# Top-32 attention feeding a mixture of experts: PSUM tiles of single banks and single heads, and natural token order for the first q and k

## The chip, the core and the metric

The kernel runs on one core of a Trainium2 chip. The time is the device time of one execution in microseconds (us). The core has five engines that each work through their own instructions in order: TensorE (PE, matmuls and transposes; PEld is its weight loads), VectorE (DVE), ScalarE (ACT), GpSimd (POOL) and SyncE (SP, which issues most DMAs). They wait for one another through semaphores. Matmuls write to PSUM, eight banks of 512 fp32 numbers in each of 128 partitions; DVE and ACT read it, POOL and DMAs don't.

## What is computed

Inputs: q, k, v of 2 batches, 8 heads, 576 tokens and 64 channels, a gate of 512 x 8, and the two weight matrices of 8 experts (512 x 1024 and 1024 x 512).

```python
scores = scale * np.matmul(q, k.transpose(0, 1, 3, 2))
kth = np.partition(scores, -top_k, axis=-1)[..., -top_k:-top_k + 1]     # top_k = 32
scores = np.where(scores >= kth, scores, -1e9)
attn = np.exp(scores - np.max(scores, axis=-1, keepdims=True))
x = (attn / attn.sum(-1)) @ v        # as 1152 tokens of 512 channels
e = np.argmax(x @ w_gate, axis=1)    # one expert for each token, at most 288 tokens each
out[i] = softmax(x @ w_gate)[i, e] * (np.maximum(x[i] @ w1[e], 0) @ w2[e])
```

## The kernel before

**Units.** The 1152 tokens make 9 blocks of 128. A unit `u` is one block and one pair of heads, 36 in all. For each unit PE makes two heads' scores of 128 x 576 (`scores`, L267); DVE takes the 8 largest of nine segments of 64 in each head (`heads`, L284) and finds from them a bound near the 32nd largest (`merge`, `bound`, L298 and L322); ACT writes the shifted scores to SBUF (`shift`, L332), which frees the scores' PSUM; ACT counts with a sign (`sign`), POOL multiplies (`turn`), DVE picks the exact threshold (`select`, L368); ACT makes a penalty for scores below it (`penalty`, L384); PE transposes scores and penalty together and ACT takes the exponential (`probs`, L393, three pieces: four 128 x 128 blocks of each head, and the last 64 columns of both heads as one block, in the tile pTt); PE multiplies with v into the tile pV (`values`, L417) and DVE divides (`normalise`).

**The order** in each engine is the order of the Python calls: the kernel schedules by hand. In the loop of `attention` (L989) iteration `i` runs `heads` and `merge` of unit `i`, `probs` of `i-3`, `values` of `i-4` and `scores` of `i+1`, so the units overlap. `routes` adds the routing steps of finished blocks (`route`, L470: transposes, gate logits, the token's expert and slot, and a scatter of the token to DRAM).

**PSUM.** The eight banks are: pD (small DVE work), pT (two buffers of one bank: transposes), pTt (one bank), pV (one bank) and pS, one tile of three banks (L270) that holds both heads' scores one behind the other, 1152 of 1536 columns. When a tile is written while another engine still has reads of it open, the writer waits; for pS the three banks count as one tile, and the next unit's scores are written when the shift of both heads has ended. At the start and in the experts the same tile serves as three banks: `tail_p` (L458) gives them out for the first transposes and the last routing, and `take_banks` (L807) puts them with pT, pD and pV into a list of seven, of which `bank` gives the next in turn.

**The start** (L121 to L176 and L1155 to L1176). SP loads q and k by pairs of heads. For the first two pairs a partition takes six successive tokens, 1,536 bytes in one piece; for the others it takes tokens 96 apart, six pieces of 256 bytes (L93). The numbers are split into a high and a low fp16 half (`split_qk`), transposed on PE (`trans_pe`) and copied to SBUF (`take`, L231) by ACT or DVE; for the first two pairs the copy also puts the tokens back in order (L234), with an output step of six elements.

**The experts** (L825). After the attention, the leftover tokens of the two fullest experts ("r", 64 each), then the other six experts in order of size: 192, 176, 144, 128, 128 and 128 tokens (L864). For each: the first layer by groups in one bank each (`h_of`), ACT's relu into `hh` (L712, L771), DVE's low half `hl` (L721, L772), the second layer (`small_y`, `ffn`), and a scatter of the result. Between the groups ACT and DVE split the next expert's weights into halves (`split_w`, L582: ACT L588, DVE and POOL L594), and SP loads further ones as buffers come free.

Of the kernel before, what the change touches and what calls it, by code (L numbers as in the profile page):

```python
# [19 lines left out]
FT = mybir.dt.float32  # L20
# [14 lines left out]
def kernel(  # L35
# [11 lines left out]
    nc = tc.nc  # L47
# [16 lines left out]
    def open_pool(key):  # L64
        P[key] = ExitStack()
        P[key, 0] = P[key].enter_context(tc.tile_pool(name=key, bufs=2, reuse_waits="tile"))
# [19 lines left out]
    def load_qk(b, p, tag="nat", names="qk"):  # L86
        for name in names:
            src = q if name == "q" else k
            XN[name, b, p] = x = (work.tile if tag == "nat" else att)([PR, 2, R, D], FT, name=name + "nat", tag=tag, bufs=4 if tag == "nat" else 2)
            for j in range(2):  # L90
                nc.sync.dma_start(x[:, j], bass.AP(
                    tensor=src.tensor, offset=src.offset + (b * H + 2 * p + j) * S * D,
                    ap=[[D, PR], [PR * D, R], [1, D]] if b or p > 1 else [[R * D, PR], [D, R], [1, D]]))  # L93
# [137 lines left out]
    def take(p, slot, j, pt, eng):  # L231
        o, pt = qk_of(0)[slot][:, 2 * p + j], pt[:, :S]
        if p < 2:
            o, pt = o.rearrange("p (t r) -> p r t", r=R), pt.rearrange("p (r t) -> p r t", r=R)  # L234
        if eng is nc.scalar:
            eng.activation(o, pt, AF.Copy)  # L236
        else:
            eng.tensor_copy(o, pt)
# [28 lines left out]
    def scores(u):  # L267
        t, p = divmod(u, HP)

        PS[u] = psum.tile([128, 3, 512], FT, name="pS", bufs=1).rearrange("p g c -> p (g c)")  # L270
        for j in range(2):
            h = 2 * p + j
            for c0, c1 in ((0, 512), (512, S)) if j == 0 else ((0, 1024 - S), (1024 - S, S)):
                for row, n, b, s in parts(t):
                    for i in range(2):
                        nc.tensor.matmul(PS[u][row:row + n, j * S + c0:j * S + c1], QK[b][2 * i][:, h, s:s + n],  # L276
                                         QK[b][1][:, h, c0:c1], start=(i == 0), stop=(i == 1))

    def scores_of(u, j):
        return PS[u][:, j * S:(j + 1) * S]  # L280
# [134 lines left out]
    PLG, PPO = pv[:, 320:328], pv[:, 384:392]  # L415
# [54 lines left out]
    def route(t, stage, eng):  # L470
        x = XR[t]
        if stage == 0:
            if TAIL_P:
                px = TAIL_P[0].rearrange("p (c t) -> p c t", c=4)
# [418 lines left out]
    def tally(i):  # L893
        PK[i] = (psum.tile([128, 128], FT, name="pTt", bufs=1), CG[:, i])
# [41 lines left out]
    def check(step):  # L936
        if step == 1:
            pf = psum.tile([128, 128], FT, name="pTt", bufs=1)
# [14 lines left out]
    def count():  # L953
        pc = psum.tile([128, 128], FT, name="pTt", bufs=1)
# [22 lines left out]
    def warm(n, few=False):  # L977
        o = psum.tile([128, 128], FT, name="pTt", bufs=1) if few else TAIL_P[2]
# [4 lines left out]
    def attention(side, early, late, mid, act, pool, end):  # L983
# [5 lines left out]
        for i in range(NU - 1):  # L989
# [82 lines left out]
        merge(L, fill)  # L1072
        tail_p()
# [80 lines left out]
    ACT, DVE, POOL = nc.scalar, nc.vector, nc.gpsimd  # L1154
    tail_p()  # L1155
# [6 lines left out]
    pt = [psum.tile([128, 1024], HF, name=f, bufs=n) for f, n in (("pT", 2), ("pT", 2), ("pTt", 1))]  # L1162
    pt += [a.bitcast(HF) for a in TAIL_P[:2]] + [pv.bitcast(HF)]
# [5 lines left out]
    TAIL_P.clear()  # L1169
    trans_qk(0, 1, 0, ACT)  # L1170
# [53 lines left out]
    close_pool("exp")  # L1224


    with tc.If(BAD[0] > 0):
        wrong = nc.values_load(flags, min_val=0, max_val=1 << 20)
        with tc.If(wrong > 0):
            open_pool("att")  # L1230
            init_xbuf(0, E * cap // 128)
# [26 lines left out]
            open_pool("exp")  # L1258
            experts_plain(0, LEAST)
            close_pool("exp")  # L1260
        more = nc.values_load(many, min_val=0, max_val=1)
        with tc.If(more > 0):
            WS.clear()
            WHICH.clear()
            open_pool("exp")
            experts_plain(LEAST, cap - LEAST)
            close_pool("exp")

# [32 lines left out]
```

## Time and profile before

| | |
|---|---|
| median of 3 runs | 434.12 us (432.04 to 436.24) |
| the profiled execution | 433.01 us, span 431.2 us |
| busy | PE 333.1, PEld 281.3, DVE 338.4, ACT 298.1, POOL 262.4 us |
| chain that ended last | DVE 55%, PE 23%, ACT 8%, issue 6%, POOL 4% |
| start, to the first maxima on DVE | 0 to 17.6 us |
| attention units | 17.6 to about 264 us |
| last routing, first expert matmuls | 264 to 302 us |
| experts | 302 to 431 us |

Busy time is the union of an engine's instructions. A row of the order of time gives start, duration, engine, line, operation, output and input tiles, and in brackets the idle time before it and the instruction that ended the wait. A busy engine is a bound only in the stretch in which it is full; elsewhere the waits tell.

### The profile page before, as it was taken

The numbers are of one execution on the slowest core, as the hardware profiler recorded it, in microseconds if no ns is written. First come the engines' busy times: TensorE is split into PE (matmuls) and PEld (weight loads), VectorE is DVE, ScalarE is ACT, GpSimd is POOL, SyncE is SP. The second block draws the span as 40 slices with busy tenths as digits, with TensorE's granted clock in tenths as the row PEclk, the third lists the DMA queues.
The fourth block names the chain that finished last, engine by engine and source line by source line (L and its number), as shares of the span: only waits on it lengthen the run. The fifth ranks groups of instructions, "written<-read, shape, count | busy, mean of one in ns | idle before, by whom it ended". The sixth has DMA issues, their size and how long they took to land.

```text
span 431.2 us, 10457 instructions
## 1 busy us (share of the span) xinstructions
PE 333.1 (77%) x3516; PEld 281.3 (65%) x3519; DVE 338.4 (78%) x1840; ACT 298.1 (69%) x553; POOL 262.4 (61%) x288
## 2 busy tenths in 40 slices
PE   4556777787877978878687898977689878895692
PEld 2334566675776757667576788973669767883571
DVE  5648999999999999999999999954427573779430
ACT  6889898898988989888896969632328543576210
POOL 5266776778885797988879799742425230548100
PEclk9559799999999999999999999999699969899698
DMA  7034989857292900000305326389589993590000
GB/s 193 1 84 110 196 227 217 189 111 113 39 286 68 346 8 27 2 2 24 100 24 183 137 39 211 120 269 338 76 301 262 281 380 84 185 291 24 0 21 22
DMA packets 66086, 60.30 MB, mean 140 GB/s; under 512 B 47461, under 2 KB 48229, under 8 KB 66023
## 3 DMA queue, kind: packets, MB, share of 16 engines
q1 hardware_dynamic: 63879, 54.79, 45.9%
q0 software_dynamic: 1616, 4.73, 3.0%
q8 instruction: 29, 0.48, 0.4%
q14 instruction: 34, 0.28, 0.2%
q10 hardware_dynamic: 528, 0.02, 0.1%
HBM read 40.66 MB, written 12.09 MB: 122 GB/s over the span
## 4 chain that ended last, share of the span: by engine, by line
DVE 55%; PE 23%; ACT 8%; issue 6%; POOL 4%; DMA 1%; SPq 0%; POOLq 0%; DVEq 0%; ACTq 0%
DVE un L291 18%; DVE z L377 10%; PE pS L633 4%; DVE ws L594 3%; ACT ws L588 3%; ACT qk L236 3%; DVE wk L314 3%; DVE pD L308 2%; DVE wk L311 2%; PE pT L728 2%; DVE pD L318 2%; PE pT L633 2%; PE pV L433 2%; PE pS L728 2%; DVE vb L316 1%
## 5 line engine op out<-in xcount | busy, mean ns | idle before, releaser
L291 DVE MAX8 un<-pS 128x8 f32<-128x64 f32 x648 | 107.4, 217 | 4.4 <-PE pS L276 4.4
L353 POOL TENSOR_TENSOR z<-sm,sg 128x576 f32<-128x576 f32 x71 | 89.4, 1279 | 29.7 <-ACT sg L346 29.4
L633 PEld LDWEIGHTS <-ws 128*128 128x128 f16 (+1 forms) x960 | 63.2, 108 | 21.8 <-issue 18.0
L594 DVE TENSOR_TENSOR ws<-wr,ws 128x1024 bf16<-128x1024 f32 x40 | 61.4, 1561 | 17.9 <-ACT ws L588 17.9
L433 PE MATMUL pV<-vm,pT 128*128 128x65 f32 (+1 forms) x640 | 73.7, 263 | 0.0
L391 ACT ACTIVATE pen<-sm,nk 128x576 bf16<-128x576 f32 x70 | 50.6, 768 | 28.9 <-DVE nk L381 28.9
L433 PEld LDWEIGHTS pV<-vm,pT 128*128 128x128 f32 (+1 forms) x640 | 69.8, 181 | 0.8
L594 POOL TENSOR_TENSOR ws<-wr,ws 128x1024 bf16<-128x1024 f32 x24 | 57.5, 2399 | 16.3 <-ACT ws L588 14.3
L276 PE MATMUL pS<-qk 128*128 128x512 f16 (+7 forms) x320 | 43.3, 293 | 29.5 <-ACT sm L336 25.5
L409 PE MATMUL pT<-identb,pen 128*128 128x128 bf16 x288 | 54.0, 225 | 13.0 <-ACT pen L391 13.0
L408 PE MATMUL pT<-ident,sm 128*128 128x128 f32 x288 | 60.2, 288 | 3.8 <-ACT xT L499 2.4
L643 POOL DMA_INDIRECT out_dram<-y,xp x12 | 14.2, 1184 | 74.6 <-DVE y L796 31.7
L276 PEld LDWEIGHTS <-qk 128*128 128x128 f16 (+1 forms) x320 | 25.4, 105 | 48.6 <-issue 32.6
L346 ACT ACTIVATE sg<-sm,mx 128x576 bf16<-128x576 f32 x72 | 54.7, 762 | 0.0
L588 ACT ACTIVATE ws<-wr 128x2048 f16<-128x2048 f32 (+1 forms) x26 | 47.6, 1844 | 6.7 <-POOL ws L594 3.3
L377 DVE MAX8 z<-z 128x8 f32<-128x576 f32 x72 | 50.8, 747 | 0.0
L336 ACT ACTIVATE sm<-pS,mx 128x576 f32<-128x576 f32 x72 | 49.1, 733 | 0.3
L408 PEld LDWEIGHTS pT<-ident,sm 128*128 128x128 f32 x288 | 42.7, 148 | 9.0 <-ACT xT L499 3.8
L633 PE MATMUL pS<-xe,ws 128*128 128x64 f16 (+7 forms) x432 | 29.8, 242 | 19.6 <-DVE hl L721 10.7
L409 PEld LDWEIGHTS <-pen 128*128 128x128 bf16 x288 | 29.8, 106 | 18.8 <-ACT pen L391 18.7
L410 ACT ACTIVATE pT<-pT 128x512 f32<-128x512 f32 x72 | 39.2, 597 | 2.6 <-PE pT L409 2.4
L781 PEld LDWEIGHTS <-ws 128*128 128x128 f16 (+1 forms) x288 | 22.6, 101 | 2.9 <-issue 2.9
(246 smaller groups left out, 661.0 us busy)
## 6 DMA issues: line engine op xcount, KB each, us to landing
wr<-in_moe_w_dram SPq DMA_DIRECT2D x32, 1024.0 KB, 6.4
xbuf<-zero SPq DMA_DIRECT2D x6, 771.0 KB, 5.5
qnat<-in_q_dram SPq DMA_DIRECT2D x16, 144.0 KB, 3.4
knat<-in_k_dram SPq DMA_DIRECT2D x16, 144.0 KB, 3.6
out_dram<-zero SPq DMA_DIRECT2D x3, 768.0 KB, 4.7
vm<-in_v_dram SPq DMA_DIRECT2D x16, 128.0 KB, 3.1
qk<-qk SPq DMA_DIRECT2D x14, 144.0 KB, 2.5
vt<-in_v_dram SPq DMA_DIRECT2D x4, 64.0 KB, 3.2
```

The lines of the kernel that those rows point to most:

```text
L276: nc.tensor.matmul(PS[u][row:row + n, j * S + c0:j * S + c1], QK[b][2 * i][:, h, s:s + n], QK[b][1][:, h, c0:c1], start=(i == 0), stop=(i ...
L291: nc.vector.max(out=un[:, j, i], in_=scores_of(u, j)[:, i * w:(i + 1) * w])
L346: nc.scalar.activation(SG[u][j], SM[u][:, j], AF.Sign, bias=VAL[u][0][:, 2, j:j + 1], scale=-(1.0 - 2.0 ** -20), accum_out=CNT[:, c:c + 1])
L353: engs[j].tensor_tensor(out=Z[u][:, j], in0=SM[u][:, j], in1=SG[u][j], op=OP.mult)
L377: nc.vector.max(out=z8[:, step - 1], in_=Z[u][:, step - 1])
L391: nc.scalar.activation(PEN[u][:, j], SM[u][:, j], AF.Relu, bias=NK[u][:, j:j + 1], scale=BIG)
L408: nc.tensor.matmul(pt[:, c], sm[:, o:o + 128], ident, start=True, stop=False, is_transpose=True)
L409: nc.tensor.matmul(pt[:, c], pen[:, o:o + 128], identb, start=False, stop=True)
L433: nc.tensor.matmul(PV[t][row:row + n, h0 + half], PT[u][:, half, c, row:row + n], VM[b][:, c, p, half], start=False, stop=(half == 1 and c ...
L588: nc.scalar.activation(w[:, 0, s], r[:, s], AF.Copy)
L594: eng.tensor_tensor(out=w[:, 1].bitcast(BF)[:, s], in0=r[:, s], in1=w[:, 0, s], op=OP.subtract)
L633: nc.tensor.matmul(o, a(i), c(i), start=(i == 0 and m == 0), stop=(i == k - 1 and m == 2))
```

## The change

1. The scores get a tile for each head: two banks, two buffers, in a PSUM pool `sc` that is open during the attention. While it is closed, the same four banks are four tiles of one bank in a pool `bk`: for the start, the last routing and the experts, whose list of banks grows from seven to eight.
2. The bank of pTt goes. The last piece of `probs` uses columns 384 to 511 of pV, the routing's logits and the counts for the experts' order use other columns of pV, and `warm`, `check` and `count` use pT.
3. In the loop all of `values` comes before the next unit's scores, and the last piece of `probs` after them.
4. The first two pairs of q and k are loaded like the others, and `take` copies in order.

```diff
@@ open_pool
+    def swap_psum(old, new):
+        if old:
+            close_pool(old)
+        open_pool(new, space=bass.MemoryType.PSUM)
@@ load_qk
-                    ap=[[D, PR], [PR * D, R], [1, D]] if b or p > 1 else [[R * D, PR], [D, R], [1, D]]))
+                    ap=[[D, PR], [PR * D, R], [1, D]]))
@@ take
-        if p < 2:
-            o, pt = o.rearrange("p (t r) -> p r t", r=R), pt.rearrange("p (r t) -> p r t", r=R)
@@ scores
-        PS[u] = psum.tile([128, 3, 512], FT, name="pS", bufs=1).rearrange("p g c -> p (g c)")
-        for j in range(2):
+        for j in js:
+            PS[u, j] = P["sc", 0].tile([128, 1024], FT, name="pS")
             h = 2 * p + j
-            for c0, c1 in ((0, 512), (512, S)) if j == 0 else ((0, 1024 - S), (1024 - S, S)):
+            for c0, c1 in ((0, 512), (512, S)):
@@ probs, j == 2
-            pt = psum.tile([128, 128], FT, name="pTt", bufs=1)
+            pt = pv[:, 384:512]
@@ tail_p
-        t = psum.tile([128, 3, 512], FT, name="pS", bufs=1)
-        TAIL_P[:] = [t[:, i] for i in range(3)]
+        TAIL_P[:] = [P["bk", 0].tile([128, 512], FT, name="bk", bufs=4) for _ in range(4)]
@@ take_banks
-        t = psum.tile([128, 3, 512], FT, name="pS", bufs=1)
+        t = [P["bk", 0].tile([128, 512], FT, name="bk", bufs=4) for _ in range(4)]
         p = [psum.tile([128, 512], FT, name="pT", bufs=2) for _ in range(2)]
-        BANKS[:] = [t[:, 0], t[:, 1], t[:, 2], p[0], pd, p[1], pv]
+        BANKS[:] = t + [p[0], pd, p[1], pv]
@@ warm
-        o = psum.tile([128, 128], FT, name="pTt", bufs=1) if few else TAIL_P[2]
+        o = psum.tile([128, 512], FT, name="pT", bufs=2)[:, :128] if few else TAIL_P[2]
@@ attention, the loop
-            exps = at(3, probs, 0) + at(3, probs, 1) + at(3, probs, 2)
+            exps, tails = at(3, probs, 0) + at(3, probs, 1), at(3, probs, 2)
             run(exps + at(0, shift) if last else at(0, shift) + exps)
-            run(routes((1, 1.5, 3)))
-            half, nxt = at(4, values, 1), at(-1, scores)
-            run(at(4, values, 0) + (half + nxt if last else nxt + half) + routes((0, 3.5)))
+            run(at(4, values) + routes((1, 1.5, 3)) + at(-1, scores) + tails + routes((0, 3.5)))
@@ after the last merge
+        swap_psum("sc", "bk")
         tail_p()
@@ the start
+    swap_psum(None, "bk")
     tail_p()
...
-    pt = [psum.tile([128, 1024], HF, name=f, bufs=n) for f, n in (("pT", 2), ("pT", 2), ("pTt", 1))]
-    pt += [a.bitcast(HF) for a in TAIL_P[:2]] + [pv.bitcast(HF)]
+    pt = [psum.tile([128, 1024], HF, name="pT", bufs=2) for _ in range(2)]
+    pt += [a.bitcast(HF) for a in (TAIL_P[3], TAIL_P[0], TAIL_P[1], pv)]
...
     TAIL_P.clear()
+    swap_psum("bk", "sc")
```

The order of the instructions shows it at three places. First ACT's first copies (`qk` is the SBUF tile for the transposed q and k, `hl` the split halves). Before:

```order
L194 ACTIVATE hl_172<-knat 96x12x64
L236 ACTIVATE qk<-pT 128x6x96 x2
L236 ACTIVATE qk<-pS 128x6x96
L236 ACTIVATE qk<-pV 128x6x96
L236 ACTIVATE qk<-pT 128x6x96 x4
L194 ACTIVATE hl_291<-knat 96x12x64
```

and now:

```order
L199 ACTIVATE hl_178<-knat 96x12x64
L239 ACTIVATE qk<-pT 128x576 x2
L239 ACTIVATE qk<-bk 128x576
L239 ACTIVATE qk<-pV 128x576
L239 ACTIVATE qk<-pT 128x576 x4
L199 ACTIVATE hl_301<-knat 96x12x64
```

The eight copies stand where they stood; their output is no longer in six interleaved parts, and what was a bank of pS is a tile bk.

Second, PE in one unit of the loop (L399 is the last piece of `probs`, L430 and L433 are `values`, L276 the next unit's scores). Before:

```order
L399 MATMUL pTt<-ident,sm 128x128
L400 MATMUL pTt<-identb,pen 128x128
L430 MATMUL pV<-vt_72,pTt 128x130
L433 MATMUL pV<-vm,pT 128x65 x4
L276 MATMUL pS<-qk 128x512
L276 MATMUL pS<-qk 128x64
L276 MATMUL pS<-qk 128x448
L276 MATMUL pS<-qk 128x128
L433 MATMUL pV<-vm,pT 128x65 x4
```

and now, with the numbers of the tiles and the semaphores waited for:

```order
L432 MATMUL pV_129<-vt0_72,pTt_1284 128x130
L435 MATMUL pV_129<-vm_92,pT_1243 128x65 x8
L278 MATMUL pS_1382<-qk_195,qk_194 128x512 [waits Activation_49]
L278 MATMUL pS_1382<-qk_195,qk_194 128x64
L278 MATMUL pS_1387<-qk_195,qk_194 128x512 [waits Activation_49]
L278 MATMUL pS_1387<-qk_195,qk_194 128x64
L401 MATMUL pV_129<-ident_104,sm_1009 128x128
L402 MATMUL pV_129<-identb_106,pen_1305 128x128
```

The second head's `values` moved ahead of the scores and the last piece behind them; the two heads' scores have a tile and a wait for ACT each.

Third, PE in the expert with 176 tokens, the first matmul of each of the four groups of its first layer (24 matmuls each). Before:

```order
L633 MATMUL pD_121<-xe_5343,ws_5707 128x176 [waits DMAHW6_49]
L633 MATMUL pS_5379<-xe_5343,ws_5707 128x176
L633 MATMUL pS_5379<-xe_5343,ws_5707 128x176 [waits DVE_49]
L633 MATMUL pS_5379<-xe_5343,ws_5707 128x176 [waits DVE_49]
```

and now:

```order
L634 MATMUL bk_5394<-xe_5355,ws_5722 128x176 [waits DMAHW6_49]
L634 MATMUL pT_5396<-xe_5355,ws_5722 128x176
L634 MATMUL pV_129<-xe_5355,ws_5722 128x176
L634 MATMUL bk_5391<-xe_5355,ws_5722 128x176
```

Three groups that shared the tile pS have tiles of their own, and the two waits for DVE are gone from these rows.

## Rows read from the trace of the kernel before

**Rows 1.** Stretches: us; busy of PE, PEld, DVE, ACT, POOL; clock; DMA.

```profile
40.80:204.00 163.20, 130.63 (x1241) 108.48 (x1239) 159.84 (x1137) 141.38 (x308) 125.58 (x137) 0.98 0.50 125
...
302.00:321.30 19.30, 14.19 (x233) 12.00 (x230) 7.60 (x8) 6.70 (x5) 5.52 (x2) 0.77 0.63 164
321.30:338.30 17.00, 16.08 (x195) 15.92 (x194) 11.33 (x10) 10.29 (x12) 7.18 (x3) 1.00 1.00 293
338.30:361.40 23.10, 18.54 (x202) 18.24 (x200) 13.13 (x12) 10.33 (x12) 6.50 (x4) 0.85 0.97 291
361.40:380.00 18.60, 15.07 (x203) 14.39 (x201) 11.61 (x12) 9.22 (x10) 7.09 (x4) 0.91 0.45 155
380.00:391.80 11.80, 11.65 (x131) 8.53 (x130) 9.79 (x9) 8.87 (x10) 8.40 (x4) 1.00 0.67 192
391.80:412.30 20.50, 12.79 (x121) 9.88 (x122) 14.00 (x10) 8.91 (x7) 6.71 (x4) 0.83 0.04 12
```

**Rows 2.** The start in order of time: start, duration, instruction, idle before it.

```profile
4.12 0.84 ACT L194 ACTIVATE hl<-qnat 96x768 f16<-96x768 f32 x1 [1.40 <-DMA qnat<-in_q_dram]
...
9.88 2.07 DVE L238 COPY qk<-pS 128x576 f16<-128x576 f16 x1
...
12.01 0.64 PE L226 MATMUL pS<-identh,hl 96*128 96x96 f16 x6 [4.42 <-DVE qk L238]
...
16.31 8.05 ACT L236 ACTIVATE qk<-pT 128x576 f16<-128x576 f16 x4
...
25.17 0.45 DVE L308 MAX8 pD<-nn 128x8 f32<-128x36 f32 x2 [4.81 <-ACT nn L333]
...
26.27 1.17 ACT L236 ACTIVATE qk<-pT 128x576 f16<-128x576 f16 x2
...
28.54 0.23 DVE L291 MAX8 un<-pS 128x8 f32<-128x64 f32 x1 [1.72 <-PE pS L276]
```

**Rows 3.** PE in the experts, in order of time: first-layer groups.

```profile
301.42 4.23 PE L633 MATMUL pS<-xe,ws 128*128 128x64 f16 x96 [2.88 <-DMA xe<-xbuf]
309.34 5.26 PE L633 MATMUL pS<-xe,ws 128*128 128x64 f16 x96 [3.70 <-DVE hl L721]
...
344.28 1.98 PE L633 MATMUL pS<-xe,ws 128*128 128x176 f16 x24 [1.35 <-DVE hl L772]
349.47 3.68 PE L633 MATMUL pS<-xe,ws 128*128 128x176 f16 x24 [3.21 <-DVE hl L772]
...
402.30 4.88 PE L633 MATMUL pS<-xe,ws 128*128 128x128 f16 x48 [6.97 <-DVE hl L721]
```

**Rows 4.** One unit of the loop in order of time, all engines.

```profile
103.07 1.37 ACT L336 ACTIVATE sm<-pS,mx 128x576 f32<-128x576 f32 x2
...
104.49 1.14 PE L276 MATMUL pS<-qk 128*128 128x512 f16 x8 [1.25 <-ACT sm L336]
...
105.47 1.06 PE L433 MATMUL pV<-vm,pT 128*128 128x65 f32 x8
...
106.30 0.22 DVE L291 MAX8 un<-pS 128x8 f32<-128x64 f32 x1
```

**Rows 5.** DMA packets from 2.5 to 6.2 us, then from 7.7 to 9.6.

```profile
DMA packets 1148, 0.90 MB, mean 243 GB/s; under 512 B 572, under 2 KB 1148, under 8 KB 1148
...
DMA packets 1953, 0.49 MB, mean 256 GB/s; under 512 B 1953, under 2 KB 1953, under 8 KB 1953
```

**Rows 6.** The last block's routing, in order of time.

```profile
286.69 0.17 DVE L515 MAX8 r<-pS 128x8 f32<-128x8 f32 x1 [2.52 <-PE pS L633]
...
288.56 0.27 ACT L525 ACTIVATE r<-pS,r 128x8 f32<-128x8 f32 x1 [2.82 <-PE pS L633]
```

**Rows 7.** ACT and DVE before the wait that ends at 402.30.

```profile
392.33 3.70 ACT L588 ACTIVATE ws<-wr 128x2048 f16<-128x2048 f32 x2
...
396.06 5.58 DVE L594 TENSOR_TENSOR ws<-wr,ws 128x1024 bf16<-128x1024 f32 x2 [0.57 <-ACT ws L588]
...
401.57 0.68 DVE L721 SCALAR_TENSOR_TENSOR hl<-pS,hh 128x512 bf16<-128x512 f32 x1
```

More of the change, by code (lines that the diff above doesn't have):

```diff
@@ L62, with open_pool @@
     P = {}
-    def open_pool(key):
+    def open_pool(key, **k):
         P[key] = ExitStack()
-        P[key, 0] = P[key].enter_context(tc.tile_pool(name=key, bufs=2, reuse_waits="tile"))
+        P[key, 0] = P[key].enter_context(tc.tile_pool(name=key, bufs=2, reuse_waits="tile", **k))
+    def swap_psum(old, new):
+        if old:
+            close_pool(old)
+        open_pool(new, space=bass.MemoryType.PSUM)
     def close_pool(key):
@@ L265, with scores @@
     PS, VAL, SM, Z, NK, PEN, PT, PTT = {}, {}, {}, {}, {}, {}, {}, {}
-    def scores(u):
+    def scores(u, js=(0, 1)):
         t, p = divmod(u, HP)
-        PS[u] = psum.tile([128, 3, 512], FT, name="pS", bufs=1).rearrange("p g c -> p (g c)")
-        for j in range(2):
+        for j in js:
+            PS[u, j] = P["sc", 0].tile([128, 1024], FT, name="pS")
             h = 2 * p + j
-            for c0, c1 in ((0, 512), (512, S)) if j == 0 else ((0, 1024 - S), (1024 - S, S)):
+            for c0, c1 in ((0, 512), (512, S)):
                 for row, n, b, s in parts(t):
                     for i in range(2):
-                        nc.tensor.matmul(PS[u][row:row + n, j * S + c0:j * S + c1], QK[b][2 * i][:, h, s:s + n],
+                        nc.tensor.matmul(PS[u, j][row:row + n, c0:c1], QK[b][2 * i][:, h, s:s + n],
                                          QK[b][1][:, h, c0:c1], start=(i == 0), stop=(i == 1))
     def scores_of(u, j):
-        return PS[u][:, j * S:(j + 1) * S]
+        return PS[u, j][:, :S]
     def heads(u, fill):
@@ L414 @@
     PVR = pv[:, :4 * (D + 1)].rearrange("p (h d) -> p h d", h=4)
-    PLG, PPO = pv[:, 320:328], pv[:, 384:392]
+    PLG, PPO = pv[:, 264:272], pv[:, 272:280]
     def values(u, half=None):
@@ L473, in route @@
             if TAIL_P:
-                px = TAIL_P[0].rearrange("p (c t) -> p c t", c=4)
+                px = TAIL_P[3 * (t % 2)].rearrange("p (c t) -> p c t", c=4)
                 plg, ppo = TAIL_P[1][:, 16 * (t % 2):][:, :E], TAIL_P[1][:, 16 * (t % 2) + 8:][:, :E]
@@ L893, in tally @@
     def tally(i):
-        PK[i] = (psum.tile([128, 128], FT, name="pTt", bufs=1), CG[:, i])
+        PK[i] = (pv[:, 280 + 8 * i:288 + 8 * i], CG[:, i])
         nc.tensor.matmul(PK[i][0][:1, :E], onesb[:, 0:1], OHS, start=True, stop=True)
@@ L937, in check @@
         if step == 1:
-            pf = psum.tile([128, 128], FT, name="pTt", bufs=1)
+            pf = psum.tile([128, 512], FT, name="pT", bufs=2)
             nc.tensor.matmul(pf[:1, 0:1], onesb[:, 0:1], fl[:, 0:1], start=True, stop=True)
@@ L953, in count @@
     def count():
-        pc = psum.tile([128, 128], FT, name="pTt", bufs=1)
+        pc = psum.tile([128, 512], FT, name="pT", bufs=2)
         nc.tensor.matmul(pc[:1, :E], onesb[:, 0:1], OHS, start=True, stop=True)
@@ L1224 @@
     close_pool("exp")
+    close_pool("bk")
     with tc.If(BAD[0] > 0):
@@ L1230 @@
             open_pool("att")
+            swap_psum(None, "sc")
             init_xbuf(0, E * cap // 128)
@@ L1258 @@
             open_pool("exp")
+            swap_psum("sc", "bk")
             experts_plain(0, LEAST)
             close_pool("exp")
+            close_pool("bk")
         more = nc.values_load(many, min_val=0, max_val=1)
@@ L1265 @@
             open_pool("exp")
+            swap_psum(None, "bk")
             experts_plain(LEAST, cap - LEAST)
             close_pool("exp")
+            close_pool("bk")
 _INS = ['q', 'k', 'v', 'moe_w_gate', 'moe_w1', 'moe_w2', 'moe_capacity']
```

## Prediction

> **What bounds the kernel now.** I read the busy time of each engine by stretch first [rows 1]. Between 40.8 and 204 us VectorE (DVE) works for 159.84 of 163.20 us: the 36 attention units run at the pace of its instructions. In the expert stretches no engine is full: DVE is busy for 7.60 of 19.30 us, 13.13 of 23.10, 11.61 of 18.60 and 14.00 of 20.50, and TensorE (PE) for 14.19, 18.54, 15.07 and 12.79, at a mean granted clock of 0.77, 0.85, 0.91 and 0.83. In the stretch from 321.3 to 338.3 us, where no expert uses the tile pS for its first layer, PE is busy for 16.08 of 17.00 us at a clock of 1.00. So something makes PE wait in four of the six stretches.
>
> The second view is the start in order of time [rows 2]. ScalarE (ACT) is the chain there. Its copies `take` with a permuted output, eight of them, cost 8.05 us for the last four, 2.01 us each; the two of the third pair, which write in order, cost 1.17 us together, 0.59 each. DVE makes two more with the permuted output, 2.07 us for the one from 9.88 on. PE waits 4.42 us to transpose the first k until DVE has copied the swapped q, although the two use different banks: both are banks of the one tile pS. DVE, done with its first maxima, waits 4.81 us, until 25.17, for ACT's `nn`, which stands behind the copies.
>
> The third view is PE's order of time in the experts [rows 3]: 3.70, 1.35, 3.21 and 6.97 us of waiting for a DVE instruction `hl` before matmuls into pS. That `hl` reads the group just finished, in another bank of the same tile. No value of it is used by the matmuls that wait: the wait is for the tile alone.
>
> The loop has its own reading [rows 4]: ACT shifts both heads' scores from 103.07 on, PE starts the next unit's eight score matmuls at 104.49, when the shift has ended, is done by 105.63, and DVE begins them at 106.30. So DVE has 0.67 us to spare, and the 3.36 us that it idles in 163.20 are all that a better order could win there.
>
> **The change, part by part.** All is counted against the profiled execution: 433.01 us, span 431.2, 1.1 us under the median of 434.12.
>
> *Start.* Eight ACT copies fall from 2.01 to 0.59 us, 11.4 us less on ACT. The two DVE copies in order have no row; the bounds are ACT's 0.59 and the 2.07 us of now, and I take 0.6, since ACT's fall with the same pattern. The wait of 4.42 us goes, because each bank is now a tile. What remains is the chain landing, split, transpose, copy. I walk it with the first q landing 0.4 us later than at 4.12 [rows 2] and k and the second pair 0.6 to 1.0 us later (below): the first k is transposed at 8.3 us instead of 12.01; DVE's split of the second q, now done when the copy starts at 9.88, ends at 10.7, its two copies at 12.0; the second q is transposed and the first scores follow from 12.0 on (about 2 us: twice the 1.14 of the eight in [rows 4], for the low clock of a start with gaps); ACT copies the second k by 15.8, splits the third k (about 1.0), and its `nn` lets DVE go on at 17.1 instead of 25.17: 8.1 us. The next scores then start after the shift of the first head (0.65 us sooner than after both) and DVE needs only the first four of eight matmuls (another 1.0): DVE begins unit 1 at 18.7 instead of 28.54, 9.8 us sooner. Units 2 and 3, where DVE still waits for scores, give another 0.7 and give back 0.5 where the matmuls that keep PE's clock up (`warm`) now wait for the copies of the transposes, whose buffers they use. I take **-10**; bounds -7 (each landing 1 us later still, copies on DVE at 2.1) and -11.4.
>
> *The loads in 256-byte pieces.* The rows decide: from 2.5 to 6.2 us, mostly pieces of 1,536 bytes, 243 GB/s; from 7.7 to 9.6 us, pieces of 256 bytes alone, 256 GB/s [rows 5]. So I expect no lower rate, and count 0.4 to 1.0 us for more pieces per tensor. The Trainium skill (DMA: Bandwidth & Descriptors, Specifications) wants at least 512 B in a transfer for the full rate; by it these loads would be slower, and the rival below says what that would cost. This trace does not agree with it: the rate of the small pieces is not the lower one.
>
> *Loop.* All of `values` now stands ahead of the scores on PE: 1.06 us of matmuls [rows 4] that stood behind. PE has waited 1.25 us at that place in this unit, so they fit. In units where PE has no such gap, scores start up to 0.7 us later, but DVE's spare time grows from 0.67 us by 0.65 (first head's shift) and 0.57 (half the matmuls), so it is covered. The last piece of the probabilities now comes behind the scores, so ACT's exponential of it comes up to 0.85 us later in the seven units with routing matmuls. Behind it on ACT stand `penalty`, `sign` and the next shift, for which PE and then DVE wait: that delay is under the 1.9 us of spare time. I count **+1** for the loop, with bounds 0 (nothing to gain where DVE is full) and +4 (all seven delays reach DVE, and the rest is lost in units 31 to 34).
>
> *Last routing.* DVE waits 2.52 us and ACT 2.82 us for matmuls of an early expert that write another bank of pS [rows 6]. Without that, the first needs the logits alone, which the same matmuls of another group delay (about 0.8 us sooner), the second what DVE wrote soon after 286.69 (1.3 us sooner). The scatter, the counting and the loads of the leftover tokens hang on this chain. I take **-1.8**, bounds -0.7 and -2.4.
>
> *Experts.* A stretch without the waits is its length less PE's idle time [rows 1], less the cold pace that follows a wait.
> - Leftover tokens, 302 to 321.3: idle 5.11; the second 96 matmuls took 5.26 us against 4.23 for the first [rows 3], 1.03 more. -6.1.
> - 338.3 to 361.4: idle 4.56 (1.35 and 3.21 are the two waits), and 24 matmuls took 3.68 against 1.98, 1.70 more. That is -6.3 if PE alone binds, -4.6 if the pace stays; the middle, -5.4, for DVE's `hl` stands behind weight splits.
> - 361.4 to 380: idle 3.53. -3.5.
> - 391.8 to 412.3: 7.71 idle. Here DVE binds next: ACT's two splits end 4.3 us into the stretch (3.70 after 0.6), DVE's two take 5.58, then `hl` 0.68 [rows 7], a split and a second `hl` (about 1.9), and PE's last quarter of the output (about 1.0): 13.5 us instead of 20.5. -7.0.
>
> Together **-22.0**. Bounds: -15 if only the four waits of [rows 3] go (15.2), -25.6 if PE alone binds (6.1 + 6.3 + 3.5 + 9.75).
>
> Sum: -10 + 1 - 1.8 - 22.0 = -32.8. From 433.0 that is 400.2, from the median 401.3. I forecast **401**.
>
> **The rivals.**
> 1. *The weights' loads become the bound.* Between 302 and 391.8 us the transfers run at 164, 293, 291, 155 and 192 GB/s in its five stretches [rows 1]: 20.0 MB. At 293 GB/s, the rate of a stretch with a share of 1.00, this takes 68 us; I leave it 89.8 - 15.0 = 75. The margin is 7 us. If the rate falls by a fifth it is gone and 10 us come back: 411. For: each load starts only when a buffer comes free. Against: no wait for weights in the trace. 0.1.
> 2. *The small pieces load at half the rate.* The first two pairs, 1.18 MB, take 4.9 us at 243 GB/s; at half the rate the last lands 4.9 us later, and most of it stands in the start's chain: 405.5. [rows 5] speak against it. 0.07.
> 3. *The expert waits only change their name.* If each group must wait for its own `hl` because ACT and DVE split weights ahead of it in order, the -22 shrinks to nothing and the start alone counts: 433.0 - 10 - 1 = 422. Against: the expert from 321.3, which has no such wait now and the same splits, keeps PE busy for 16.08 of 17.00 us. 0.06.
> 4. *Slower.* The late piece makes ACT the bound of the loop: ACT waits for PE, PE for ACT's next shift, in every unit. It costs 34 us, and so all the gain, when each of 32 units grows by 1.06 us, the whole of the moved matmuls. From 1.06 us a unit on the kernel is slower: 434 to 436. Against: DVE's spare time of 1.9 us would have to go first. 0.04.
>
> **The numbers.** Forecast 0.73 (395 to 407), the rivals 0.10, 0.07, 0.06 and 0.04. The range of 8 in 10, with the bounds of the start and of the experts in it, is 393 to 412. A change of 1% is about what a measurement of this kernel can tell from none: faster by more 0.93, within 1% 0.03, slower 0.04.
>
> **What would show it.** In the changed profile: copies `take` of about 0.6 us and PE without the wait of 4.42; DVE's first wait for `nn` ending near 17 us; DVE as full in the loop as now, its waits for scores under 4.4 us; no wait of PE for `hl` before first-layer matmuls; the four expert stretches at about 13, 17.5, 15 and 13.5 us with a clock above 0.9. The prediction is wrong if DVE idles in the loop, if ACT's splits wait for loads, or if the experts' stretches keep their length.

## The result and the profile after

The changed kernel takes 410.67 us in the median of 4 runs (410.09 to 411.32), beside 433.08 us for the kernel before: a ratio of 0.9476, with a 95% interval of 0.9414 to 0.9538. The forecast was 401 us, the range 393 to 412. So the time lies inside the range near its upper end; of the 32.8 us of gain that the sum gave, 23.0 us came, counted in the spans of the two profiled executions (431.2 and 408.2 us). The ratios leave out executions over 1.5% above the fastest of their kernel, and the profiles of experiment 2 and of the routing's order in experiment 6 show such executions.

The loss is found by following both traces in order of time. Units are counted from 0, as in the prediction. A table of how far the changed kernel is ahead at the same instruction:

| place | before, us | after, us | ahead | change of the lead | forecast |
|---|---|---|---|---|---|
| first maxima of unit 4 (DVE) | 47.19 | 36.53 | 10.66 | 10.66 | 10 |
| end of the last maxima (DVE) | 263.76 | 255.38 | 8.38 | -2.28 | -1 |
| last block's logits (PE) | 285.28 | 280.56 | 4.72 | -3.66 | 0 |
| scatter of the last tokens (POOL) | 290.60 | 285.13 | 5.47 | +0.75 | +1.8 |
| leftover tokens, first matmul (PE) | 301.42 | 296.86 | 4.56 | -0.91 | 0 |
| last scatter of results (POOL) | 424.12 | 402.01 | 22.11 | +17.55 | +22.0 |

Three steps carry it: 3.7 us lost behind the last maxima, where the prediction had nothing; 4.5 us too little in the experts; 1.3 us in the loop. Another 2.0 us are missing between the last block's logits and the leftover tokens, and 1.6 us came back at the start and behind the last scatter. The start gave what was expected.

The experts by stretch, after (length; busy of PE, PEld, DVE, ACT, POOL; clock; DMA), in the same order as the last six rows of [rows 1]:

```profile
296.86:309.60 12.74, 12.73 (x241) 9.87 (x241) 6.89 (x7) 6.70 (x5) 5.40 (x2) 0.87 0.86 185
309.60:326.50 16.90, 15.98 (x194) 15.83 (x193) 12.61 (x12) 10.50 (x12) 7.29 (x3) 1.00 1.06 317
326.50:344.35 17.85, 15.76 (x204) 15.47 (x202) 13.40 (x12) 10.11 (x12) 6.56 (x4) 1.00 1.06 376
344.35:362.90 18.55, 14.84 (x204) 14.57 (x202) 13.61 (x12) 9.80 (x12) 7.18 (x4) 0.91 0.68 192
362.90:374.30 11.40, 11.35 (x131) 8.56 (x130) 9.44 (x9) 8.57 (x7) 8.06 (x3) 1.00 0.71 190
374.30:390.04 15.74, 12.51 (x120) 7.74 (x120) 15.74 (x10) 8.86 (x7) 8.75 (x5) 0.89 0.04 16
```

The forecast had about 13 us for the leftover tokens, 17.5 for the expert of 176 tokens, 15 for that of 144 and 13.5 for the second of 128. The first two came (12.74 and 17.85). The other two took 18.55 and 15.74, and the clock stayed under the forecast's 0.9 in two (0.87 and 0.89). In the last of them DVE is busy for all of 15.74 us, where the prediction had counted about 13.5 for the whole chain.

PE in these stretches, in order of time:

```profile
296.86 7.48 PE L634 MATMUL bk<-xe,ws 128*128 128x64 f16 x192 [3.59 <-DMA xe<-xbuf]
...
346.72 4.66 PE L634 MATMUL bk<-xe,ws 128*128 128x144 f16 x72
357.19 0.22 PE L782 MATMUL bk<-hl,ws 128*128 128x144 bf16 x1 [2.75 <-DVE hl L773]
...
386.63 3.62 PE L729 MATMUL pT<-ws,hl 128*128 128x512 f16 x8 [3.12 <-DVE hl L722]
```

No first-layer matmul (L634) waits for `hl` any more: the 192 of the leftover tokens run in one piece where [rows 3] had two of 96 and 3.70 us between them. The wait for `hl` now stands at the second layer (L782, L729), which reads `hl`: a wait for a value, not for a tile. What makes `hl` late is seen on DVE and POOL, from both engines' order of time:

```profile
350.66 6.11 DVE L595 TENSOR_TENSOR ws<-wr,ws 128x1024 bf16<-128x1024 f32 x2 [0.73 <-ACT ws L589]
356.69 0.45 DVE L773 SCALAR_TENSOR_TENSOR hl<-bk,hh 128x288 bf16<-128x288 f32 x1
...
350.44 2.17 POOL L595 TENSOR_TENSOR ws<-wr,ws 128x1024 bf16<-128x1024 f32 x1
352.86 2.83 POOL L595 TENSOR_TENSOR ws<-wr,ws 128x1024 bf16<-128x1024 f32 x1 [0.25 <-POOL ws L595]
...
371.93 14.05 DVE L595 TENSOR_TENSOR ws<-wr,ws 128x1024 bf16<-128x1024 f32 x5
385.89 0.68 DVE L722 SCALAR_TENSOR_TENSOR hl<-pT,hh 128x512 bf16<-128x512 f32 x1
```

DVE's two pieces of weight splits take 6.11 us, while POOL makes two pieces of the same kind beside them; five take 14.05. Elsewhere in the same trace a single one takes 1.21.

Behind the last maxima, PE, ACT and DVE in order of time (L523 makes the routing's counts in pV, L401 and L402 the last piece of the probabilities in other columns of pV, L403 is its exponential, L528 reads the counts):

```profile
257.55 0.21 PE L523 MATMUL pV<-oh,tri 128*128 128x8 bf16 x1
...
260.79 0.28 PE L401 MATMUL pV<-ident,sm 128*128 128x128 f32 x1
...
261.48 0.27 ACT L403 ACTIVATE pTt<-pV 128x128 f32<-128x128 f32 x1
...
261.85 0.17 DVE L528 SCALAR_TENSOR_TENSOR r<-pV,oh 128x8 f32<-128x8 f32 x1 [3.86 <-ACT pTt L403]
```

The counts are there at 257.8 us, but DVE reads them at 261.85: 3.86 us of waiting for another piece of the same tile. Behind L528 on DVE stand the thresholds of the last two units, and so their penalties and probabilities.

### The profile page after: what moved, and what is told of

Read it like the earlier page. It is cut to its first block, busy times and chain, and to the rows that moved or that the text cites. A ratio compares the mean times of both kernels' runs of the same rounds, so it can differ in the third digit from the quotient of the medians.

```text
span 408.2 us, 10423 instructions
## 1 busy us (share of the span) xinstructions
PE 331.5 (81%) x3516; PEld 275.6 (67%) x3519; DVE 341.7 (84%) x1840; ACT 287.5 (70%) x553; POOL 262.7 (64%) x288
## 4 chain that ended last, share of the span: by engine, by line
DVE 50%; PE 30%; ACT 7%; issue 7%; DMA 3%; SPq 1%; POOL 0%; ACTq 0%; DVEq 0%; POOLq 0%
DVE un L293 16%; DVE z L379 8%; DVE ws L595 5%; PE pV L435 5%; PE bk L634 4%; PE pT L729 3%; PE pS L278 3%; PE pT L410 2%; DVE wk L316 2%; DVE pD L310 2%; DVE pD L320 2%; DVE wk L313 2%; ACT ws L589 2%; PE pT L634 1%; DMA xp<-xbuf 1%
## 5 line engine op out<-in xcount | busy, mean ns | idle before, releaser
L355 POOL TENSOR_TENSOR z<-sm,sg 128x576 f32<-128x576 f32 x71 | 89.5, 1279 | 31.2 <-ACT sg L348 30.9
L411 PE MATMUL pT<-identb,pen 128*128 128x128 bf16 x288 | 56.5, 231 | 35.9 <-ACT pen L393 34.7
L595 DVE TENSOR_TENSOR ws<-wr,ws 128x1024 bf16<-128x1024 f32 x40 | 65.9, 1678 | 13.7 <-ACT ws L589 13.6
L435 PE MATMUL pV<-vm,pT 128*128 128x65 f32 (+1 forms) x640 | 69.3, 266 | 0.0
L435 PEld LDWEIGHTS pV<-vm,pT 128*128 128x128 f32 (+1 forms) x640 | 68.6, 186 | 0.0
L410 PE MATMUL pT<-ident,sm 128*128 128x128 f32 x288 | 63.0, 297 | 4.6 <-ACT xT L500 2.6
L595 POOL TENSOR_TENSOR ws<-wr,ws 128x1024 bf16<-128x1024 f32 x24 | 56.6, 2360 | 12.2 <-ACT ws L589 10.6
L634 PEld LDWEIGHTS <-ws 128*128 128x128 f16 (+1 forms) x960 | 56.2, 100 | 5.4 <-issue 4.8
L644 POOL DMA_INDIRECT out_dram<-y,xp x12 | 17.1, 1424 | 60.6 <-DVE y L797 29.0
L278 PE MATMUL pS<-qk 128*128 128x512 f16 (+3 forms) x320 | 45.3, 298 | 4.0 <-ACT sm L338 4.0
L634 PE MATMUL bk<-xe,ws 128*128 128x64 f16 (+9 forms) x480 | 27.1, 219 | 3.6 <-DMA xe<-xbuf 3.6
L782 PEld LDWEIGHTS <-ws 128*128 128x128 f16 (+1 forms) x288 | 23.0, 103 | 7.4 <-issue 7.4
```

The costliest lines, as they stand in the source:

```text
L278: nc.tensor.matmul(PS[u, j][row:row + n, c0:c1], QK[b][2 * i][:, h, s:s + n], QK[b][1][:, h, c0:c1], start=(i == 0), stop=(i == 1))
L355: engs[j].tensor_tensor(out=Z[u][:, j], in0=SM[u][:, j], in1=SG[u][j], op=OP.mult)
L410: nc.tensor.matmul(pt[:, c], sm[:, o:o + 128], ident, start=True, stop=False, is_transpose=True)
L411: nc.tensor.matmul(pt[:, c], pen[:, o:o + 128], identb, start=False, stop=True)
L435: nc.tensor.matmul(PV[t][row:row + n, h0 + half], PT[u][:, half, c, row:row + n], VM[b][:, c, p, half], start=False, stop=(half == 1 and c ...
L595: eng.tensor_tensor(out=w[:, 1].bitcast(BF)[:, s], in0=r[:, s], in1=w[:, 0, s], op=OP.subtract)
```

## The experiments

Every kernel is the changed one with the edit shown. In two more groups the changed kernel ran beside them:

> The changed kernel once more, as it is, beside the others of this group, so that differences of 2 us to it can be told: 409 to 412 us.

> The changed kernel a third time, beside the others of this group: 410 to 412 us.

They gave 411.96 us (408.11 to 413.68; ratio to before 0.9499, 0.9458 to 0.9540) and 413.73 us (410.31 to 414.68; 0.9526, 0.9490 to 0.9561). Medians of the same kernel differ by up to 3 us between groups, so an edit is compared with the changed kernel of its own group where that ran. Experiments 1, 2, 4 and the first run of 3 have none beside them.

**1. The start undone** (the fourth part of the change).

```diff
-                    ap=[[D, PR], [PR * D, R], [1, D]]))
+                    ap=[[D, PR], [PR * D, R], [1, D]] if b or p > 1 else [[R * D, PR], [D, R], [1, D]]))
...
+        if p < 2:
+            o, pt = o.rearrange("p (t r) -> p r t", r=R), pt.rearrange("p (r t) -> p r t", r=R)
```

> The changed kernel with its fourth part undone: the first two pairs of q and k are loaded as six successive tokens per partition again, and the copies put the tokens back in order. Theory: the start's gain of 10.66 us (first maxima of unit 4 at 36.53 us instead of 47.19) comes from this part and reaches the end whole: 420 to 422 us, copies of about 2.0 us. Rival A: half of it comes from the tiles of single banks, which stay (no 4.42 us wait of PE): 415 to 417 us. Rival B: the small pieces of the loads cost something that returns here: under 415 us.

Measured: 421.31 us (417.04 to 425.68), 419.59 by the executions that the ratio counts; ratio 0.9683 (0.9569 to 0.9796). ACT's copies, first of this kernel, then of the changed one:

```profile
6.72 4.05 ACT L241 ACTIVATE qk<-pT 128x576 f16<-128x576 f16 x2 [0.51 <-PE pT L231]
...
7.01 1.19 ACT L239 ACTIVATE qk<-pT 128x576 f16<-128x576 f16 x2 [0.32 <-PE pT L231]
```

Two copies take 4.05 against 1.19 us. The first maxima of unit 4 start at 43.40 us, 6.9 later than in the changed kernel's profile and 8.0 later than in that of its first repetition (35.38), but 3.8 sooner than before. So in the start about two thirds of the gain come from the fourth part and a third from the single banks: the theory gave the fourth part all of it, rival A half. From 419.59 us the part is worth 5.9 to 8.9 us, depending on the group of the changed kernel. The two profiles differ by 9.6 us in span, of which 2.4 come in the experts, which the edit doesn't touch.

**2. One tile for the experts' four banks.**

```diff
-        t = [P["bk", 0].tile([128, 512], FT, name="bk", bufs=4) for _ in range(4)]
+        t = P["b4", 0].tile([128, 4, 512], FT, name="b4", bufs=1)
+        t = [t[:, i] for i in range(4)]
```

> The changed kernel, but in the experts the four banks that became free are one tile again, so that a write into one waits for the reads of all. Theory: the waits of PE for hl before first-layer matmuls return, and the experts from the leftover tokens to the last scatter take 117 to 123 us instead of 105.1: 422 to 428 us. Rival (the waits only changed their name, and ACT's and DVE's weight splits bind anyway): under 4 us more, 411 to 415 us.

Measured: 431.98 us (428.58 to 436.92, 10 runs), ratio 0.9973 (0.9933 to 1.0013). The kernel is as slow as before the change, though the start keeps its lead (first maxima of unit 4 at 35.35 us). PE's waits in the experts, in us in all, times, longest:

```profile
PE b L782 <- DVE hl L773: 7.4, 2, 6.4
PE b L634 <- DVE hl L773: 5.2, 2, 3.6
...
PE b L634 <- DVE hl L722: 2.0, 1, 2.0
```

The first-layer waits (L634) are back, and waits at the second layer with them. The experts take 126.5 us instead of 105.1, more than the theory's upper end and more than the 122.7 of the kernel before: in these profiles a tile of four banks is worse than the tile of three. In units 14 to 16 of the loop, which the edit doesn't touch, that profile has 6.3 us more than the changed kernel's first repetition (clock 0.53 from 104 to 122 us); this is no part of the 126.5. The false wait is confirmed as what the experts' part of the change removes.

**3. A bank of their own for the last pieces, behind the last maxima.**

```diff
-            pt = pv[:, 384:512]
+            pt = TAIL_P[2][:, :128] if TAIL_P else pv[:, 384:512]
```

> The changed kernel, but after the last merge the last pieces of the probabilities go to a bank of their own instead of columns 384 to 511 of pV. Theory: the 4 us that the stretch behind the last maxima lost (8.4 us ahead of before at the last maxima, 4.7 us ahead at the last block's logits) are DVE's 3.86 us wait to read the routing's counts in pV, a wait for the exponential of another piece of the same tile. It goes, PE stays warm, and the kernel takes 406.5 to 408 us. Rival: PE, busy for 23.2 of 25.1 us there, is the bound, and the wait goes to the next reader of pV: 410 to 411 us.

Measured: 410.86 us (408.12 to 411.82), ratio 0.9484 (0.9422 to 0.9546): no gain in the median. But in its profile the wait of L528 is gone and the way from the last maxima to the scatter of the last tokens takes 25.4 us instead of 29.7 (257.30 to 282.74 against 255.38 to 285.13). The loop lost what this won. Two stretches of that profile's loop:

```profile
200.00:205.00 5.00, 5.00 (x26) 3.90 (x25) 3.92 (x26) 2.37 (x5) 3.51 (x3) 0.50 0.00 0
...
230.00:235.00 5.00, 5.00 (x26) 3.90 (x26) 3.22 (x27) 1.43 (x3) 3.69 (x3) 0.50 0.08 32
```

TensorE is at half clock for both (0.50, 1.2 GHz), and DVE, otherwise busy for 4.9 of 5 us, for 3.92 and 3.22. Units 28, 29, 32 and 33 are 4.2 us longer together than in the changed kernel's profile, and unit 31 is 0.5 us shorter. The edit does not touch the loop, so the kernel ran again, beside the changed one:

> The kernel with the last pieces of the probabilities in a bank of their own after the last merge, again, now beside the changed kernel on the same chip. Its profile showed the way from the last maxima to the last scatter of tokens 4.3 us shorter, its median nothing. Theory: the gain is real and stretches at half TensorE clock in the loop hid it: 2.5 to 4 us less than the changed kernel beside it. Rival: the way after the last maxima gives it back in each execution: within 1 us of it.

Measured: 409.76 us (408.00 to 412.85) against 413.73 in the same group, ratios 0.9447 (0.9408 to 0.9486) and 0.9526 (0.9490 to 0.9561). The wait is 4.84 us in that group's changed kernel and absent here:

```profile
259.74 0.17 DVE L528 SCALAR_TENSOR_TENSOR r<-pV,oh 128x8 f32<-128x8 f32 x1 [4.84 <-ACT pTt L403]
...
256.21 0.17 DVE L528 SCALAR_TENSOR_TENSOR r<-pV,oh 128x8 f32<-128x8 f32 x1
```

The way to the scatter is 27.1 us against 30.9. So the wait is gone in every trace with the edit, and the way is shorter by 4.3, 3.8 and (experiment 6 below) 2.7 us; the median of this group shows 4.0. The first group's median does not show it. The reason given for that, half clock in the loop, stands in this profile and, in the same units, in that of experiment 8 (clock 0.50 from 200 to 205 and from 230 to 235 us), while in those of experiment 6 and of the second run here these units are not longer. For the other executions behind the median it is not shown.

**4. DVE makes all weight pieces in the experts.**

```diff
-            split_w(e, i, c, half, nc.gpsimd if (g, half) in ((0, 1), (2, 1)) else nc.vector, 1)
+            split_w(e, i, c, half, nc.vector, 1)
```

> The changed kernel, but in the experts DVE makes the two pieces of each weight split that POOL made. Theory: DVE and POOL hold each other up in these instructions (a DVE piece takes 1.21 us alone and up to 5.62 us where pieces of POOL lie beside it); all DVE pieces take 1.21 us then, the 2.75 and 3.12 us of PE's waits for hl in the experts of 144 and 128 tokens shrink, and the kernel takes 404 to 408 us. Rival: the long pieces have another cause and DVE is short of time: two pieces more, 2.4 us in each of the stretches where DVE comes last, 413 to 416 us.

Measured: 403.87 us (403.24 to 407.71), ratio 0.9337 (0.9260 to 0.9415). DVE does 12 pieces more and is faster. The group of these instructions (busy us, mean ns | idle before), in the changed kernel, in this one, and in number 7 below:

```profile
L595 DVE TENSOR_TENSOR ws<-wr,ws 128x1024 bf16<-128x1024 f32 x40 | 65.9, 1678 | 13.7 <-ACT ws L589 13.6
...
L595 DVE TENSOR_TENSOR ws<-wr,ws 128x1024 bf16<-128x1024 f32 x52 | 61.1, 1217 | 14.2 <-ACT ws L589 14.1
...
L595 DVE TENSOR_TENSOR ws<-wr,ws 128x1024 bf16<-128x1024 f32 x28 | 66.5, 2387 | 16.1 <-ACT ws L589 15.3 <-issue 0.7
```

52 pieces take 61.1 us, 40 took 65.9. By the ratios of the three groups of the changed kernel the edit is worth 6 to 8 us. The stretch with 144 tokens falls to 14.65 us, within the forecast's 15. The second with 128 tokens stays at 15.76, for another reason, on POOL, ACT and PE:

```profile
358.35 11.44 POOL L644 DMA_INDIRECT out_dram<-y,xp  x1 [10.40 <-DVE y L797]
...
371.86 0.69 ACT L759 ACTIVATE y<-bk,xp 128x512 f32<-128x512 f32 x1 [7.70 <-issue]
...
376.68 1.90 PE L729 MATMUL pT<-ws,hh 128*128 128x512 f16 x8 [3.50 <-ACT hh L713]
```

A scatter, about 1 us alone, lies on POOL for 11.44 us beside DVE's pieces. The outputs share two buffers; ACT seems to wait for the one that this scatter reads, for the trace shows nothing else that it could wait for, and PE then waits for ACT's relu. Experiment 8 tries this.

**5. The loop in its old order.**

```diff
-            exps, tails = at(3, probs, 0) + at(3, probs, 1), at(3, probs, 2)
+            exps = at(3, probs, 0) + at(3, probs, 1) + at(3, probs, 2)
...
-            run(at(4, values) + routes((1, 1.5, 3)) + at(-1, scores) + tails + routes((0, 3.5)))
+            run(routes((1, 1.5, 3)))
+            half, nxt = at(4, values, 1), at(-1, scores)
+            run(at(4, values, 0) + (half + nxt if last else nxt + half) + routes((0, 3.5)))
```

> The changed kernel with the loop's order of before: the last piece of the probabilities ahead of the values, the second half of the values behind the scores. Theory: the new order is what makes the shared tile pV affordable; in the old order the values wait for ACT's exponential of the last piece, 1 to 1.5 us in each unit, most of it covered by DVE's 1.9 us to spare: 410.5 to 414 us. Rival A: the order itself costs the loop its 2.3 us: 408.5 to 409.5 us. Rival B: the wait is not covered, 1 us in each of 32 units: above 430 us.

Measured: 512.51 us (511.71 to 520.78), ratio 1.1810 (1.1756 to 1.1865). Rival B came, at more than three times its price. From unit 12 to 34, the longest waits:

```profile
DVE un L293 <- PE pS L278: 52.1, 22, 4.5
...
PE pV L432 <- ACT pTt L403: 28.3, 11, 3.5
```

PE's values wait up to 3.5 us in a unit for the exponential of the last piece. My estimate had only ACT's exponentials in it; ahead of them on ACT stand `nn` and the shift of both heads too, and the next scores come behind the values. TensorE's clock fell too, to 0.72 in these units against 0.95 in the changed kernel's profile, so the 100 us need not all be waiting for ACT; no run parts the two. So the third part of the change is not a cost of its own that could be saved: it is the condition under which the last piece can share pV with the values.

**6. The routing's matmuls behind the scores, and both edits (3 and 4) together.**

```diff
-            run(at(4, values) + routes((1, 1.5, 3)) + at(-1, scores) + tails + routes((0, 3.5)))
+            run(at(4, values) + at(-1, scores) + routes((1, 1.5, 3)) + tails + routes((0, 3.5)))
```

> The changed kernel, but in the loop the routing's matmuls (logits, transposes, counts) come behind the next unit's scores instead of ahead of them. Theory: the units 15, 23, 27 and 31, each 0.26 to 0.32 us longer than before, are so because scores wait for values and logits on TensorE; they return to 6.86 us, 1.2 us together: 409 to 410 us. Rival: these units are longer for another reason, or the routing now comes too late: no gain, 410.5 to 412 us.

Measured: 412.11 us (408.20 to 418.47) against 411.96 beside it: no gain, the rival. The group's changed kernel also shows why: there, units 14, 22 and 26 (15, 23 and 27 in the expectation, which counts from 1) take 6.86, 6.85 and 6.86 us without any edit. The 0.3 us in each that I had read as the price of the order come with half clock in the unit before, where an execution has it there.

> Both edits that were tried alone: the last pieces of the probabilities after the last merge in a bank of their own, and the expert weights' pieces of POOL on DVE. Theory: the two are in different stretches and add up, 3.9 us off the 403.9 of the second alone: 399 to 401 us. Rival: whatever kept the first from showing in the median (its own profile lost 3.4 us in units 29 to 34, at half TensorE clock) is there again: 402.5 to 404.5 us.

Measured: 402.87 us (400.37 to 405.49), ratio 0.9293 (0.9245 to 0.9341), 1.0 us under edit 4 alone, in another group: within the rival's range, not the theory's. Its profile has the way behind the last maxima 2.7 us shorter than that of edit 4 alone (27.1 against 29.7).

**7. POOL makes four of eight pieces.**

```diff
-nc.gpsimd if (g, half) in ((0, 1), (2, 1)) else nc.vector
+nc.gpsimd if half else nc.vector
```

> The changed kernel, but POOL makes four of the eight pieces of each weight split instead of two, so that the suspected cost is doubled. Theory: a DVE piece that starts while a piece of POOL runs waits until that one ends; there are twice as many, so the pieces that stay on DVE take 2 us and more on average and the experts get longer although DVE has two pieces less: 414 to 422 us. Rival: DVE gains from the relief: 405 to 410 us.

Measured: 419.73 us (416.69 to 421.17), ratio 0.9656 (0.9606 to 0.9706), 6.0 us slower than the changed kernel beside it. DVE's pieces take 2,387 ns each (last row of the group above). One of them, and what lies beside it on POOL:

```profile
355.92 9.27 DVE L595 TENSOR_TENSOR ws<-wr,ws 128x1024 bf16<-128x1024 f32 x1 [0.73 <-issue]
...
355.70 8.39 POOL L595 TENSOR_TENSOR ws<-wr,ws 128x1024 bf16<-128x1024 f32 x4
```

DVE's piece starts 0.22 us after POOL's first and ends 1.10 us after POOL's fourth, about its own length: as if it had stood still in between.

**8. Both edits, and two more buffers for the outputs.**

```diff
-            y = work.tile([128, Dm], FT, name="y", tag="xr", bufs=2)
+            y = P["exp", 0].tile([128, Dm], FT, name="y", tag="y", bufs=2)
```

> Both edits (own bank after the last merge, POOL's pieces on DVE) and two buffers of their own for the outputs y that finish writes, where all outputs of the experts shared two. Theory: in the run with both edits a scatter on POOL lay 11.45 us beside DVE's pieces, ACT waited 7.68 us to write the next y into the buffer that the scatter still read, and PE 3.50 us for the relu behind it; with more buffers ACT and PE don't wait: 399 to 401 us against 402.9. Rival: DVE's pieces end no earlier and PE's wait goes to hl: 402 to 404 us.

Measured: 398.97 us (396.20 to 400.25), ratio 0.9172 (0.9134 to 0.9210): the fastest of all, 14.8 us under the changed kernel beside it. The scatter still takes 11.45 us, but nobody waits for it. The second stretch with 128 tokens:

```profile
368.19:379.95 11.76, 10.90 (x122) 7.54 (x121) 10.38 (x11) 8.86 (x7) 4.22 (x3) 1.00 0.14 45
```

11.76 us, where the changed kernel took 15.74 and the forecast had 13.5. All experts together take 96.2 us (295.75 to 391.93).

## Why the prediction was right in direction and 10 us too low

The time lies in the range, but outside the 395 to 407 us to which the prediction gave 0.73. It lies beside the 411 of rival 1, whose mechanism did not happen: that nearness is chance. Term by term:

**Start, -10: 10.66, right in mechanism, the sum with some luck.** Unit 1 starts at 17.18 us, a lead of 11.36 where 9.8 was worked out; of this 0.70 is given back by unit 4, where the prediction had 0.2 more to come. In the two repetitions the lead at unit 4 is 11.8 and 12.5 us. The copies take 0.59 to 0.65 us on ACT and 0.4 on DVE, PE no longer waits for DVE's copy, and DVE's first wait for `nn` ends at 15.38 us (forecast 17.1):

```profile
4.43 0.84 ACT L199 ACTIVATE hl<-qnat 96x768 f16<-96x768 f32 x1 [1.72 <-DMA qnat<-in_q_dram]
...
9.28 0.81 DVE L241 COPY qk<-bk 128x576 f16<-128x576 f16 x2
...
15.38 0.45 DVE L310 MAX8 pD<-nn 128x8 f32<-128x36 f32 x2 [0.75 <-ACT nn L335]
```

**Loads in small pieces: the cost was small, but the rate is lower, which the prediction did not expect.** ACT begins to split the first q 0.31 us later (4.43 against 4.12), the first k 0.01 later (5.85 against 5.84); against experiment 1, which loads in long pieces, it is 0.29 and 0.47 us. From 2.5 to 6.2 us, now in pieces of 256 bytes:

```profile
DMA packets 3510, 0.80 MB, mean 216 GB/s; under 512 B 3510, under 2 KB 3510, under 8 KB 3510
```

216 GB/s against 243 in [rows 5]: a ninth less, not half. Rival 2 did not happen. The Trainium skill's demand for 512 B at least (DMA: Bandwidth & Descriptors, Specifications) agrees in sign with this row, where the prediction had seen no agreement in the trace before.

**Loop, +1: 2.28 in this execution.** DVE is as full as before, 204.64 of 209.70 us. Eight of its units (13, 14, 21, 22, 25, 26, 29 and 30) are 1.5 us longer together than before, each pair with a stretch at half clock (1.2 GHz) in its first unit, and unit 31 gives back 0.25. In the repetition of the same kernel, at full clock there, the same units take what they took before. The stretch of units 29 and 30, first in the changed kernel, then in its repetition:

```profile
205.00:210.00 5.00, 4.19 (x28) 3.76 (x28) 4.93 (x34) 5.00 (x11) 3.19 (x6) 0.66 0.00 0
...
205.00:210.00 5.00, 4.50 (x43) 3.75 (x42) 4.86 (x35) 4.84 (x12) 4.35 (x3) 1.00 0.00 0
```

What is left is 0.34 us in unit 34 and 0.68 in the last unit, 0.57 of it a wait of DVE for a piece in pV, the same sharing as behind the loop: the forecast's 1. In both repetitions the way from unit 4 to the end of the maxima is 1.0 us longer than before. Rival 4 did not happen: with the late piece ACT is not the bound. It is the old order, in experiment 5, that makes PE wait for ACT, at more than 3 us a unit (232.7 us from unit 12 to unit 34, against 151.1).

**Behind the last maxima: the missing term.** The sum had no entry there. The prediction looked at the second part of the change (the bank of the last piece goes) only inside the loop, where the order was rewritten with it. Behind the last maxima the order is written out by hand and was left as it was, and there DVE reads the counts behind the last piece. The same rule by which I found the false waits in pS, one tile, several uses, would have found this one in pV: 3.86 us of wait, 3.66 of lost lead.

**Last routing, -1.8: 0.75.** The logits' maxima came 0.76 sooner, as worked out. The second step (1.3) didn't:

```profile
283.09 0.27 ACT L526 ACTIVATE r<-bk,r 128x8 f32<-128x8 f32 x1 [2.07 <-PE bk L524]
```

This exponential needs the logits and what DVE wrote by 281.85 us, but the counts (L523, L524), of which it reads nothing, go into the same bank, and it still waits for them. The change parts the banks of pS, not these two users of one bank. Here the wait is the longer because `oh`, which the counts read, took 0.92 us instead of 0.23 beside a POOL instruction (L512, 281.61 to 282.77). No run gave the counts a bank of their own.

**Experts, -22.0: 17.55.** The waits for the tile are gone, and the leftover tokens (-7.2 against -6.1) and the expert with 176 tokens (-5.3 against -5.4) are as worked out. Rivals 1 and 3 did not happen: in these stretches no engine waits for weights, and the waits that came instead are smaller. The failed step is the durations on DVE. For 361.4 to 380 I took all of PE's idle time as gain, and for 391.8 to 412.3 I took the 5.58 us for two pieces from [rows 7] as a fixed price. That row itself spoke against it: 2.8 us each, where a piece alone takes 1.21. The pieces are long where POOL works beside them. That the splits of DVE and POOL move closer together when PE no longer waits is read from the two traces (the longest piece took 3.17 us before and 5.62 now). Over the 40 pieces the excess over 1.21 us grew from 14 us (1,561 ns each before) to 18.7 us (1,678). Experiments 4 and 7 show it by taking the cause away and by doubling it.

**What was argued only.** That the 0.91 us lost between the last scatter of tokens and the leftover tokens' first matmul belong to the loads of `xe` is read from one wait (3.59 us against 2.88); over all profiles this way takes 10.8 to 12.6 us, and no run was made for it. The change also gives the transposes of the last two blocks two banks in turn; no run parts this off.

## What to carry to other kernels

Where a PSUM tile has several banks or several users, list for every write and read which open access of the same tile it must wait for, also in the code that the change does not touch: a split that removes false waits in one tile can put them into the next (pS to pV). Before a stretch is priced by subtracting a wait, see whether the instructions that come next have a fixed duration; two rows of the same form with different lengths (1.21 and 2.8 us) say that they don't. A shared resource on the helper engine (POOL) can cost more than the work it takes over: here giving 12 pieces back to DVE won 6 to 8 us.

## What the runs showed of the hardware

**DVE and POOL exclude each other in these instructions.** A DVE subtraction of two SBUF tiles of 128x1024 takes 1.21 us alone (mean 1,217 ns over 52 pieces), 5.62 beside two POOL pieces, 9.27 beside four; a POOL scatter takes 1.0 us alone, and 11.4 beside eight pieces of DVE. So the one who waits can be passed over by several instructions running, not one. The Trainium skill (SBUF — State Buffer, "SBUF: two separate sides") states that the two share a pair of ports as an exclusive lock, taken by a DVE operation with two SBUF inputs (against a GpSimd operation that reads SBUF) and held for the whole instruction, and that a DMA issued from GpSimd starves behind DVE (told there for DVE's two-port mode). The rows agree on the lock; that a scatter is held up behind this two-input operation too is shown by the rows here.

**The clock differs between executions of one kernel.** In the changed kernel's profiles TensorE stands at half clock (1.2 GHz) at different places of the loop, without any edit there. The four stretches in the loop of the first profile go with 0.3 to 0.4 us each, one in unit 28 of the first repetition with nothing. In the two rows of 0.50 in experiment 3 DVE works 2.6 us less than in the changed kernel's rows of the same times (3.92 and 3.22 us against 4.86 in both); before each fall PE was busy for 3.0 and 3.4 of 5 us. Differences of 2 to 3 us between medians of this kernel can't be told without a control in the same group.
